# Attention and two feed-forward networks: the rational function of network 2 moved into PSUM banks, one of its products to GpSimd

## The chip, the core and the metric

One core of a Trainium2 chip runs the whole program in one launch. The metric is the device time of one execution in microseconds. TensorE (PE) multiplies matrices into PSUM, which has eight banks of 128 x 512 fp32; VectorE (DVE) and ScalarE (ACT) work elementwise on PSUM and SBUF; GpSimd (POOL) works elementwise on SBUF; SyncE (SP) issues all the transfers, one queue in program order.

## The reference, cut to what matters

```python
def reference(q, k, v, moe_*, moe2_*):
    x = attention(q, k, v)              # chunks of 64, 8 x 8 heads x 576 rows -> 4608 x 512
    h = x @ w_in;  g = relu(h) ** 2     # network 1: 512 -> 2048
    x = g @ w_out                       #            2048 -> 512
    h = x @ w_in2                       # network 2: 512 -> 2048
    P = a[0] + a[1]*h + a[2]*h**2 + a[3]*h**3
    Q = 1.0 + abs(b[0])*abs(h) + abs(b[1])*h**2
    g = P / (Q + 1e-6)
    return (g @ w_out2)                 #            2048 -> 512, 4608 x 512 out
```

## The kernel before

The 4608 rows are nine blocks of 512. Each fp32 operand is held as a high part and a low part, and each product of two of them is three matmuls of 128 x 512 (`mm3`: low by high, high by low, high by high). A "tile" is one 128 x 512 piece of h, `(b, f)` for block b and feature slice f of 16, so a network has 144 tiles; a "second product" is the 12 matmuls that take one finished tile g through `w_out` into the four `acc` banks. Network 1 runs its first product tile by tile (12 matmuls in `mm_h`), and the second product two tiles later (`mm_out1`). Network 1's last 16 second products (`BACK = 16`) are put off: their activations are kept in SBUF (`keep`, 20 slots in the space of weights that are no longer needed), the last 14 first products run back to back, and the 16 are done inside network 2.

Network 2 takes eight of the nine blocks in four pairs. For a pair `m` and a pair of feature slices `u` (a "unit", 32 of them) seven products of sums replace eight (`mm_p`, numbered 1 to 7, 6 matmuls each; the sums of weights lie in `w2q`, those of the inputs in `x2q`). From them come four tiles of h: 11 (products 1 and 2), 12, 22 and 21. Before, the order of TensorE in a unit is 1, 5, second product, 6, 2, second, 7, 3, second, 4, second, with no second products in unit 0; the ninth block follows in `mm_s2` (16 tiles of 12 matmuls, each with a second product), and the 20 second products that are left end the program.

The parts of a tile are put together so: products 1, 6, 7 and 4 go on one after the other in one bank (`h`, two buffers), 5 and 3 in `e`, 2 in `b`. ScalarE copies the running sums to SBUF where they branch off (`q_copy`: `s1`, `s5`, `sU`), VectorE adds them (`q_add`): 11 into its own bank `b`, 12 and 22 into SBUF (`h12`, `h22`); 21 is left in bank `h`. Then comes the rational function, eleven instructions a tile: ScalarE's square (L905), scaled abs (L909) and affine (`id`, L917); VectorE's denominator `t` (L913, both inputs in SBUF); ScalarE's ln and exp for the reciprocal (L921, L925); VectorE's `wh`, `wa` (L929, L933, which read h), `u` (L937, a Newton step on the reciprocal), `wr` (L941) and `g` (L944, which ends it into a kept slot). For the second product ScalarE makes the high part of g (`o_hi`, `gh`) and GpSimd the low part (`o_lo`, `gl`, L196).

For the next pair of blocks GpSimd forms the sums of the inputs from rows loaded back from DRAM: per `xq` (24 of them in network 2, eight per pair, in a pair's first five units) a load, four subtractions (L344), ScalarE's high part, GpSimd's low part (L196) and a store, in one buffer `xroom`.

The order of network 2 on all queues is made by a planner (`job`, `plan`): TensorE's order is given, every other engine takes of what is ready by the planner's own costs what is due first, and the result is a fixed order for each queue. In `issue` the events of one common list are written out in order of their time.

Of the kernel before, what the change touches and what calls it, by code (L numbers as in the profile page):

```python
# [19 lines left out]
NB = 512  # L20
# [8 lines left out]
COST = {"sq": 2.6, "abs": 3.0, "id": 3.4, "ln": 3.2, "exp": 3.2, "hi": 2.8, "cp": 2.8, "t": 3.7, "wh": 3.0, "wa": 3.3,  # L29
        "u": 3.0, "wr": 3.3, "g": 3.1, "add": 3.2, "lo": 5.7, "ev": 2.8}  # L30
# [52 lines left out]
def attn_moe_moe_kernel(  # L83
# [43 lines left out]
    h_p = ctx.enter_context(tc.tile_pool(name="hps", bufs=2, space=PSUM))  # L127
# [150 lines left out]
    def w2_parts(key, st, x):  # L278
# [9 lines left out]
        copy(nc.scalar, hi, x)  # L288
# [34 lines left out]
    def xq_room(i):  # L323
# [3 lines left out]
        z = (T["xroom"] if i >= 8 else T["room", i % 2])[:, 0:14 * 128].rearrange("p (x t j) -> p t x j", t=2, j=128)  # L327
# [42 lines left out]

    def mm_h(s):
# [6 lines left out]
        ps = h_p.tile([128, 512], F32, name="h", tag="h")  # L378
# [3 lines left out]
    def mm_h_half(s, i, k):  # L382
# [3 lines left out]
        if i == 0 and k == 0:  # L386
            T["h", s] = h_p.tile([128, 512], F32, name="h", tag="h")
# [29 lines left out]
    def mm_out2(s, g):  # L417
# [3 lines left out]
        for i in range(TPB):  # L421
# [4 lines left out]
            for j in PARTS:  # L426
                T["rest", j.start] = h_p.tile([128, 512], F32, name="h", tag="h")
# [144 lines left out]
    def mm_pv2(*ts):  # L572
        o = [h_p.tile([128, 512], F32, name="h", tag="h").rearrange("p (t b i) -> p t b i", t=2, i=64) for _ in range(2)]
# [79 lines left out]
    def g_tr(g, nm):  # L653
        x = T.pop((nm, "group", g))
        ps = h_p.tile([128, 2, 2, 128], F32, name="h", tag="h")
# [136 lines left out]
    def t2(nm):  # L792
        return tl("t2", [128, NB], F32, nm)
# [7 lines left out]
    free = list(range(20))  # L801

    def slot(i):
        return spare(i // 2)[:, i % 2]
# [18 lines left out]
    def x_page(i, c):  # L823
# [5 lines left out]
        return X[0][i - 7][:, 2 * c:2 * c + 2] if i < 9 else T["xmore"][c]  # L829
# [14 lines left out]
    def xs_hi(i, c):  # L844
        need("ring_x", i, 2)
# [7 lines left out]
    def bank(tag):  # L853
        return (h_p if tag == "h" else P["eb"]).tile([128, 512], F32, name="h", tag=tag)

    def mm_p(m, u, p):
        i, j = 7 * m + ORDER.index(p), 7 * (8 * m + u) + ORDER.index(p)
# [4 lines left out]
        tag, first = {1: "h", 5: "e", 2: "b"}.get(p), True  # L862
        if tag is None:
            tag, first = "e" if p == 3 else "h", False
        else:
            T[tag] = bank(tag)
        w = i_tile(j).rearrange("p (t k j) -> p t k j", t=2, k=2)
        x = [x_page(i, c) for c in range(2)]
        for c in range(2):
            mm3(T[tag], [([w[:, t, c] for t in range(2)], [x[c][:, t] for t in range(2)])], first and c == 0, c == 1, p in (6, 3, 7, 4))  # L870
# [5 lines left out]
    def mm_s2(f):  # L876
        u, i = divmod(f, 2)
        j = 7 * NF // 2 * (NBLK // 2) + 4 * u + 2 * i
        ps = bank("h")
# [565 lines left out]
```

## Time and profile before

| | us |
|---|---|
| median of 3 runs (lowest to highest) | 1722.89 (1719.42 to 1723.58) |
| the profiled execution, its own time | 1720.5 |
| its span, first to last instruction | 1718.7 |
| PE busy over the span | 1623.8 |
| DVE busy | 1282.6 |
| ACT busy | 983.9 |
| POOL busy | 558.2 |

The profiled execution's time is 1.8 us longer than its span and 2.4 us under the median of the runs. An engine's busy time counts its instructions alone, not its waits. An average over the span hides that the program has parts with different limits: attention and network 1 until 820 us, network 2 after that. A matmul that is listed with 0.39 us overlaps the next one; what counts is the distance from start to start. Some matmul records can be missing, so counts of them are lower bounds.

### The profile page before, as it was taken

The page shows a single profiled execution, that of the slowest core. Times are in us where ns is not written, and L with a number is a line of the kernel's source. Part 1 is how long each engine was busy: PE and PEld are TensorE (multiplying, and loading weights), DVE is VectorE, ACT ScalarE, POOL GpSimd, SP SyncE. Part 2 cuts the span into 40 slices and gives each one's busy share as a digit, 9 for nine tenths or more (in the row PEclk, how much of TensorE's full clock was granted, in tenths as well). Part 3 has the DMA queues.
Part 4 walks back from the last instruction along what each step waited for, and adds up shares of the span by engine and source line. Part 5 has one row for each costly group of instructions (what it writes and reads, how often), then busy time and mean ns, then how long its engine had stood idle before and what let it go on. Part 6 is the DMA issues. An engine that isn't in the chain of part 4 may idle for free.

```text
span 1718.7 us, 25720 instructions
## 1 busy us (share of the span) xinstructions
PE 1623.8 (94%) x9165; PEld 1323.7 (77%) x9165; DVE 1282.6 (75%) x1869; ACT 983.9 (57%) x1619; POOL 558.2 (32%) x463
## 2 busy tenths in 40 slices
PE   8999999999999999999988896999988999998999
PEld 7888778888878888888767675777766777777887
DVE  7886566666666666630799997999998999999970
ACT  6853343344333433334767775777767777777752
POOL 4640212212202112241345434552555333222233
PEclk9999999999999999999999999999999999999999
DMA  9755653444445354449868796888977886565644
GB/s 261 202 131 158 215 146 99 134 107 134 111 115 155 81 147 112 144 122 308 278 209 261 243 319 208 246 260 308 289 238 227 281 298 217 173 195 164 209 138 156
DMA packets 358871, 335.18 MB, mean 195 GB/s; under 512 B 195288, under 2 KB 269272, under 8 KB 357720
## 3 DMA queue, kind: packets, MB, share of 16 engines
q1 hardware_dynamic: 358744, 333.54, 63.7%
q8 instruction: 73, 1.20, 0.3%
q14 instruction: 54, 0.44, 0.1%
HBM read 251.66 MB, written 81.79 MB: 194 GB/s over the span
## 4 chain that ended last, share of the span: by engine, by line
PE 49%; DVE 34%; DMA 5%; ACT 4%; issue 3%; POOL 2%; SPq 1%; DVEq 0%; POOLq 0%; ACTq 0%
PE acc L367 8%; PE acc L368 8%; PE acc L369 8%; PE h L367 8%; PE h L369 7%; PE h L368 7%; DVE t L913 5%; DVE spare L944 5%; DVE w L941 4%; DVE w L929 4%; DVE w L933 4%; DVE t L937 4%; DVE at L641 3%; DVE h L898 2%; DMA x2q<-xroom 2%
## 5 line engine op out<-in xcount | busy, mean ns | idle before, releaser
L196 POOL TENSOR_TENSOR gl<-spare,gh 128x512 fp32r<-128x512 f32 x160 | 235.7, 1481 | 439.1 <-ACT gh L191 415.0
L367 PE MATMUL h<-x,w 128*128 128x512 f32 (+1 forms) x792 | 311.4, 393 | 22.1 <-ACT sU L191 10.5
L368 PE MATMUL h<-x,w 128*128 128x512 f32 (+1 forms) x792 | 308.6, 390 | 0.3 <-DVE x L196 0.3
L369 PE MATMUL h<-x,w 128*128 128x512 f32 (+1 forms) x792 | 308.5, 390 | 0.0
L367 PE MATMUL acc<-w,gl 128*128 128x512 f32 x575 | 226.8, 394 | 14.3 <-POOL gl L196 13.6
L367 PE MATMUL acc<-gh,w 128*128 128x512 f32 x576 | 227.8, 395 | 4.0 <-ACT ev L191 2.3
L368 PE MATMUL acc<-gl,w 128*128 128x512 f32 x576 | 225.1, 391 | 0.8 <-POOL gl L196 0.6
L368 PE MATMUL acc<-w,gh 128*128 128x512 f32 x575 | 225.7, 392 | 0.0
L369 PE MATMUL acc<-w,gh 128*128 128x512 f32 x575 | 225.5, 392 | 0.0
L369 PE MATMUL acc<-gh,w 128*128 128x512 f32 x576 | 224.7, 390 | 0.0
L478 ACT ACTIVATE r<-h 128x512 f32<-128x512 f32 x128 | 76.0, 594 | 208.3 <-PE h L369 148.1
L367 PEld LDWEIGHTS h<-x,w 128*128 128x128 f32 x792 | 149.7, 189 | 58.7 <-ACT sU L191 13.0
L193 DVE CAST gh<-r 128x512 fp32r<-128x512 f32 x120 | 56.6, 472 | 184.3 <-ACT r L479 183.8
L196 POOL TENSOR_TENSOR st<-wc,st 128x512 fp32r<-128x512 f32 x32 | 49.4, 1544 | 411.7 <-ACT st L191 330.4
L369 PEld LDWEIGHTS h<-x,w 128*128 128x128 f32 x792 | 149.7, 189 | 30.7
L368 PEld LDWEIGHTS h<-x,w 128*128 128x128 f32 x792 | 149.9, 189 | 30.4 <-DVE x L196 0.5
L913 DVE SCALAR_TENSOR_TENSOR t<-h,co,t 128x512 f32<-128x512 f32 x144 | 142.9, 992 | 19.0 <-ACT t L909 18.8
L921 ACT ACTIVATE r<-t,co 128x512 f32<-128x512 f32 x144 | 103.7, 720 | 82.3 <-DVE t L913 81.8
L944 DVE SCALAR_TENSOR_TENSOR spare<-t,w 128x512 f32<-128x512 f32 x144 | 128.7, 894 | 16.5 <-DVE w L941 1.4
L367 PEld LDWEIGHTS acc<-w,gl 128*128 128x128 f32 x575 | 109.3, 190 | 41.1 <-POOL gl L196 16.6
L941 DVE SCALAR_TENSOR_TENSOR w<-w,co,r 128x512 f32<-128x512 f32 x144 | 139.6, 969 | 0.0
L367 PE MATMUL h<-w,w 128*128 128x512 f32 x240 | 100.2, 418 | 41.0 <-DVE h L898 15.8
(141 smaller groups left out, 3166.3 us busy)
## 6 DMA issues: line engine op xcount, KB each, us to landing
w<-w2o SPq DMA_DIRECT2D x144, 512.0 KB, 4.9
w<-w2q SPq DMA_DIRECT2D x256, 256.0 KB, 3.9
x2q<-xroom SPq DMA_DIRECT2D x24, 896.0 KB, 5.2
st<-in_moe_w_in_dram SPq DMA_DIRECT2D x32, 512.0 KB, 4.9
st<-in_moe_w_out_dram SPq DMA_DIRECT2D x32, 512.0 KB, 5.5
w2q<-st SPq DMA_DIRECT2D x32, 512.0 KB, 2.9
w<-x2q SPq DMA_DIRECT2D x30, 512.0 KB, 8.8
x<-x2q SPq DMA_DIRECT2D x22, 512.0 KB, 8.9
```

The source lines that it names most:

```text
L196: eng.tensor_tensor(out=o, in0=x, in1=hi.bitcast(F32), op=ALU.subtract)
L367: nc.tensor.matmul(out=o, lhsT=al, rhs=bh, start=first and i == 0, stop=False, **kw)
L368: nc.tensor.matmul(out=o, lhsT=ah, rhs=bl, start=False, stop=False, **kw)
L369: nc.tensor.matmul(out=o, lhsT=ah, rhs=bh, start=False, stop=last and i == len(pairs) - 1, **kw)
L478: nc.scalar.activation(out=r, in_=ps, func=ACTF.Relu)
L913: eng.scalar_tensor_tensor(out=t, in0=T.pop(("h2", b, f)), scalar=co[:, 5:6], in1=t, op0=ALU.mult, op1=ALU.add)
L921: nc.scalar.activation(out=T["r", b, f], in_=T["t", b, f], func=ACTF.Ln, scale=2.0 ** -LN_SHIFT, bias=co[:, 6:7])
L929: nc.vector.tensor_tensor(out=w, in0=w, in1=T["H", b, f], op=ALU.mult)
L933: nc.vector.scalar_tensor_tensor(out=w, in0=w, scalar=co[:, 1:2], in1=T.pop(("H", b, f)), op0=ALU.add, op1=ALU.mult)
L937: nc.vector.scalar_tensor_tensor(out=u, in0=u, scalar=1.0 + 1e-6, in1=T["r", b, f], op0=ALU.add, op1=ALU.mult)
L941: nc.vector.scalar_tensor_tensor(out=w, in0=w, scalar=co[:, 0:1], in1=T.pop(("r", b, f)), op0=ALU.add, op1=ALU.mult)
L944: nc.vector.scalar_tensor_tensor(out=keep("g", BACK + b * NF + f), in0=T.pop(("t", b, f)), scalar=2.0, in1=T.pop(("w", b, f)), op0=ALU.sub ...
```

## The change

Nothing changes in attention and in network 1's arithmetic. In network 2:

- The four banks that the products use become four equal ones, and a table of roles (`role`, `NEXT`) says which bank serves as h, e, b or g in which unit. A branching sum is begun by a copy from bank to bank (`q_fork`: ScalarE copies product 1 from h into b; product 2 is then accumulated on it), and one sum is written by VectorE from bank h to bank e (`q_v`), on which product 3 is accumulated. One copy to SBUF (`s5`) is left. Tile 22 is written by VectorE into the bank with role g (`q_22`). So a unit has two ScalarE copies for three, and two VectorE adds for three.
- All four tiles of h stay in PSUM. The reciprocal is written by exp over h in its bank, `wr`, `u` and `g` read it there, and the bank is handed on only when `g` is done. In the tile with role g alone (`R_SB`) it is written to SBUF and the bank is free after `wa`.
- The denominator is |h| times (b1 |h| + b0): ScalarE does abs and an affine (`q_abs`, `q_lin`), and GpSimd the product (`q_q`), in place of ScalarE's square and abs and VectorE's `t`. VectorE has five instructions a tile for six.
- Every second high part of g is made on GpSimd and not on ScalarE (`"AG"[n % 2]`).
- 20 second products of network 1 are put off and not 16, all units have four second products, unit 0 too, and the order in a unit is 1, second, 5, 6, 2, second, 3, 7, second, 4, second. There are 23 kept slots, three buffers each of `r`, `t`, `w` in pools of their own, and two of `xroom`; the ring of x pages has 9 places for 10.
- The planner has other costs, due times for transfers that follow from TensorE's order, and a longer lead for a load of `xq` (`X_LAT`).
- In network 1, 48 copies that make high parts of network 2's weights go from ScalarE to GpSimd, and one activation in 16 tiles is written later.

```diff
-BACK = 16
-RING_O, RING_I, RING_X = 6, 12, 10
-ORDER = 1, 5, 6, 2, 7, 3, 4
+BACK = 20
+RING_O, RING_I, RING_X = 6, 12, 9
+UNIT_SEQ = "1o562o37o4o"
+ORDER = [int(x) for x in UNIT_SEQ if x != "o"]
+NEXT = {"h": "b", "e": "e", "b": "g", "g": "h"}
+R_SB = "g"
...
-    def q_copy(nm, tag):
-        T[nm] = tl("sx", [128, NB], F32, nm)
-        copy(nc.scalar, T[nm], T[tag])
-
-    def q_add(tag, nm, b, f):
-        o = T[tag] if tag == "b" else tl("sx", [128, NB], F32, {"e": "h12", "h": "h22"}[tag])
-        nc.vector.tensor_tensor(out=o, in0=T[tag], in1=T.pop(nm), op=ALU.add)
...
+    def q_fork(un, src, o):
+        T[o] = bank(role(un, o))
+        copy(nc.scalar, T[o], T[src])
+    def q_s5():
+        T["s5"] = tl("s5", [128, NB], F32, "s5")
+        copy(nc.scalar, T["s5"], T["e"])
+    def q_v():
+        nc.vector.tensor_tensor(out=T["e"], in0=T["h"], in1=T["s5"], op=ALU.add)
+    def q_22(un, b, f):
+        T["H", b, f] = bank(role(un, "g"))
+        nc.vector.tensor_tensor(out=T["H", b, f], in0=T["h"], in1=T.pop("s5"), op=ALU.add)
...
-    def q_t(b, f, eng):
         t = T["t", b, f]
-        eng.scalar_tensor_tensor(out=t, in0=T.pop(("h2", b, f)), scalar=co[:, 5:6], in1=t, op0=ALU.mult, op1=ALU.add)
...
+        nc.gpsimd.tensor_tensor(out=t, in0=t, in1=T["r", b, f], op=ALU.mult)
...
+    def q_exp(b, f, in_place=True):
+        r, h = T["r", b, f], T.pop(("H", b, f))
+        if in_place:
+            T["r", b, f] = h
+        nc.scalar.activation(out=T["r", b, f], in_=r, func=ACTF.Exp, scale=-1.0, bias=co[:, 7:8])
...
-            due = nominal[x] - 4
+            due = nominal[x] - 12
...
-            made["hi", n] = job("A", COST["hi"], src + prev + buf, due - 7, o_hi, n, nc.scalar)
+            eng = "AG"[n % 2]
...
+                made["hi", n] = job(eng, COST["hi"], src + prev + buf, due - 8, o_hi, n, engines[eng])
...
-                    q_ = [(made["xq", i - 1], D_LAT)] if i > 8 else []
+                    q_ = [(made["xq", i - 2], X_LAT)] if i > 9 else []
```

What stands on VectorE in the middle of network 2, before (`spare` is a kept slot, `r`, `t`, `w` are the function's own tiles, `h` with a number is a tile of h in SBUF, and `h` alone one in PSUM or SBUF):

```order
L913 SCALAR_TENSOR_TENSOR t<-h_12347,co,t 128x512
L929 TENSOR_TENSOR w<-w,h_12304 128x512
L933 SCALAR_TENSOR_TENSOR w<-w,co,h_12304 128x512
L913 SCALAR_TENSOR_TENSOR t<-h_12401,co,t 128x512
L937 SCALAR_TENSOR_TENSOR t<-t,r_12413 128x512
L941 SCALAR_TENSOR_TENSOR w<-w,co,r_12413 128x512
L944 SCALAR_TENSOR_TENSOR spare_8088<-t,w 128x512
```

And now, over two tiles, the second with role g:

```order
L946 TENSOR_TENSOR w<-w,h 128x512
L950 SCALAR_TENSOR_TENSOR w<-w,co,h 128x512
L963 SCALAR_TENSOR_TENSOR w<-w,co,h 128x512
L967 SCALAR_TENSOR_TENSOR h<-t,h 128x512
L970 SCALAR_TENSOR_TENSOR spare_7920<-h,w 128x512
L963 SCALAR_TENSOR_TENSOR w<-w,co,r 128x512
L967 SCALAR_TENSOR_TENSOR r<-t,r 128x512
L970 SCALAR_TENSOR_TENSOR spare_7920<-r,w 128x512
```

The row of `t` is gone, and of a tile's last three rows each has one operand in the bank `h` where it had two in SBUF; the tile with role g keeps two in SBUF.

On GpSimd in the same part before, only low parts and the work for the next pair of blocks stand in a row (`xroom`: sums L344 and low part L196):

```order
L196 TENSOR_TENSOR gl<-spare_8088,gh 128x512
L344 TENSOR_TENSOR xroom<-xroom 128x128 x4
L196 TENSOR_TENSOR gl<-spare_8192,gh 128x512
L196 TENSOR_TENSOR xroom<-xroom 128x7x128
L196 TENSOR_TENSOR gl<-spare_8269,gh 128x512
```

Now (L942 is the denominator's product, L199 the high part):

```order
L942 TENSOR_TENSOR t<-t,r 128x512
L350 TENSOR_TENSOR xroom_8056<-xroom_8056 128x128 x4
L202 TENSOR_TENSOR gl<-spare_8118,gh 128x512
L199 CAST gh<-spare_8190 128x512
L202 TENSOR_TENSOR xroom_8056<-xroom_8056 128x7x128
L942 TENSOR_TENSOR t<-t,r 128x512
```

The product of a tile stands behind the sums and the low part of the next pair's inputs, which begin with a load.

On TensorE, at the start of network 2, before: product 1 is followed by product 5 (`x_71` and `x_72` hold x pages, `w_0` a page of sums of weights):

```order
L367 MATMUL h<-x_71,w_0_76 128x512
L368 MATMUL h<-x_71,w_0_76 128x512
L369 MATMUL h<-x_71,w_0_76 128x512
L367 MATMUL h<-x_72,w_0_76 128x512
L368 MATMUL h<-x_72,w_0_76 128x512
L369 MATMUL h<-x_72,w_0_76 128x512
```

Now:

```order
L373 MATMUL h<-x_71,w_0_76 128x512
L374 MATMUL h<-x_71,w_0_76 128x512
L375 MATMUL h<-x_71,w_0_76 128x512
L373 MATMUL acc_580<-gh,w_4_8006 128x512
L374 MATMUL acc_580<-gl,w_4_8006 128x512
L375 MATMUL acc_580<-gh,w_4_8006 128x512
```

A second product of network 1 stands between them. In all, 48 matmuls fewer stand ahead of network 2's first.

## Rows read from the trace of the kernel before

**Rows 1.** Busy time by stretch: length, then engine busy (instructions), granted clock, DMA share, GB/s.

```profile
100.00:750.00 650.00, 642.43 (x4469) 528.13 (x4469) 408.18 (x748) 250.62 (x426) 127.14 (x111) 1.00 0.48 132
860.00:1400.00 540.00, 477.28 (x1994) 380.67 (x1993) 501.71 (x613) 391.95 (x634) 248.87 (x202) 0.97 0.81 260
1400.00:1600.00 200.00, 186.89 (x792) 151.86 (x793) 190.45 (x253) 153.86 (x251) 58.37 (x39) 0.97 0.61 198
1600.00:1714.00 114.00, 114.00 (x506) 94.53 (x505) 60.93 (x74) 57.25 (x92) 37.85 (x29) 1.00 0.48 159
```

**Rows 2.** Timeline of PE: start, length; network 2's first and last matmul.

```profile
817.81 0.39 PE L367 MATMUL h<-x,w 128*128 128x512 f32 x1
...
820.53 0.39 PE L367 MATMUL h<-x,w 128*128 128x512 f32 x1
...
1714.28 0.28 PE L369 MATMUL h<-w,gh 128*128 128x256 f32 x1
```

**Rows 3.** Waits of PE, 820 to 1719: us in total, times, longest.

```profile
PE h L367 <- ACT sU L191: 23.3, 13, 3.7
PE h L367 <- DVE h L898: 19.4, 12, 10.8
```

**Rows 4.** DVE's groups, 860 to 1500: count | busy us, mean ns | idle before.

```profile
L941 DVE SCALAR_TENSOR_TENSOR w<-w,co,r 128x512 f32<-128x512 f32 x107 | 100.4, 938 | 0.0
...
L898 DVE TENSOR_TENSOR h<-h,s 128x512 f32<-128x512 f32 x54 | 36.7, 686 | 1.8 <-PE h L369 1.8
```

**Rows 5.** Timeline of all engines, 1120 to 1125: DVE beside POOL.

```profile
1120.35 1.30 POOL L196 TENSOR_TENSOR gl<-spare,gh 128x512 fp32r<-128x512 f32 x1
...
1120.45 0.69 DVE L898 TENSOR_TENSOR h<-h,sU 128x512 f32<-128x512 f32 x1
...
1121.60 2.58 POOL L196 TENSOR_TENSOR xroom<-xroom 128x896 fp32r<-128x896 f32 x1
...
1122.11 2.62 DVE L941 SCALAR_TENSOR_TENSOR w<-w,co,r 128x512 f32<-128x512 f32 x1
```

**Rows 6.** Timeline of DVE, 1129 to 1132, where POOL does nothing.

```profile
1129.97 0.75 DVE L941 SCALAR_TENSOR_TENSOR w<-w,co,r 128x512 f32<-128x512 f32 x1
1130.83 0.69 DVE L944 SCALAR_TENSOR_TENSOR spare<-t,w 128x512 f32<-128x512 f32 x1
1131.43 0.68 DVE L929 TENSOR_TENSOR w<-w,h 128x512 f32<-128x512 f32 x1
```

**Rows 7.** ACT's groups, 860 to 1500.

```profile
L921 ACT ACTIVATE r<-t,co 128x512 f32<-128x512 f32 x107 | 77.1, 720 | 65.4 <-DVE t L913 65.0
...
L191 ACT ACTIVATE s<-h 128x512 f32<-128x512 f32 x52 | 30.0, 588 | 0.0
```

**Rows 8.** POOL's groups over the span.

```profile
L344 POOL TENSOR_TENSOR xroom<-xroom 128x128 f32<-128x128 f32 x96 | 63.8, 683 | 93.2 <-DMA xroom<-x2d 84.9 <-issue 6.4
L196 POOL TENSOR_TENSOR xroom<-xroom 128x896 fp32r<-128x896 f32 x24 | 58.8, 2449 | 15.9 <-ACT xroom L191 14.9 <-PE acc L369 1.1
...
L704 POOL TENSOR_TENSOR e<-e,z 128x512 f32<-128x512 f32 x2 | 2.1, 1044 | 11.1 <-DVE z L699 10.7 <-ACT x L191 0.4
L193 POOL CAST gh<-r 128x512 fp32r<-128x512 f32 x3 | 1.9, 639 | 6.6 <-ACT r L479 6.6
```

**Rows 9.** Timelines of SP, POOL and PE round the longest stall; in brackets idle before.

```profile
1052.36 8.23 SPq L821 DMA_DIRECT2D w<-w2q  x1
...
1068.33 1.81 POOL L344 TENSOR_TENSOR xroom<-xroom 128x128 f32<-128x128 f32 x4 [12.86 <-DMA xroom<-x2d]
...
1074.59 0.79 PE L367 MATMUL h<-w,w 128*128 128x512 f32 x1 [10.79 <-DVE h L898]
```

**Rows 10.** SP's timeline ahead of network 2, first and last loads of x pages.

```profile
798.74 0.95 SPq L839 DMA_DIRECT2D x<-x2q  x2
...
808.73 12.31 SPq L839 DMA_DIRECT2D w<-x2q  x8
```

**Rows 11.** Waits of POOL on the loads of xroom, 820 to 1600: us, times, longest.

```profile
POOL xroom L344 <- DMA xroom<-x2d: 84.9, 15, 12.9
```

More of the change, by code (lines that the diff above doesn't have):

```diff
@@ L572, in mm_pv2 @@
     def mm_pv2(*ts):
-        o = [h_p.tile([128, 512], F32, name="h", tag="h").rearrange("p (t b i) -> p t b i", t=2, i=64) for _ in range(2)]
+        o = [h_bank().rearrange("p (t b i) -> p t b i", t=2, i=64) for _ in range(2)]
         for i, t in enumerate(ts):
@@ L799, in part @@
         return ALL if i < 0 else PARTS[i]
-    free = list(range(20))
+    free = list(range(20 + MORE))
     def slot(i):
-        return spare(i // 2)[:, i % 2]
+        return spare(i // 2)[:, i % 2] if i < 20 else T["more"][:, i - 20]
     def keep(what, n):
@@ L861, in mm_p @@
         need("ring_x", i, 2)
[L862 to L866, printed above, removed]
+        tag = {2: "b", 5: "e", 3: "e"}.get(p, "h")
+        if p in (1, 5):
+            T[tag] = bank(role(un, tag))
         w = i_tile(j).rearrange("p (t k j) -> p t k j", t=2, k=2)
@@ L869, in mm_p @@
         for c in range(2):
-            mm3(T[tag], [([w[:, t, c] for t in range(2)], [x[c][:, t] for t in range(2)])], first and c == 0, c == 1, p in (6, 3, 7, 4))
+            mm3(T[tag], [([w[:, t, c] for t in range(2)], [x[c][:, t] for t in range(2)])], p in (1, 5) and c == 0, c == 1, p not in (1, 5))
+        if p == 2:
+            T["H", 2 * m + 1, 2 * u] = T.pop("b")
+        if p == 3:
+            T["H", 2 * m, 2 * u] = T.pop("e")
         if p == 4:
@@ L878, in mm_s2 @@
         j = 7 * NF // 2 * (NBLK // 2) + 4 * u + 2 * i
-        ps = bank("h")
+        ps = bank(role(NF // 2 * (NBLK // 2) - 1, "begh"[f % 4]))
         pairs = []
@@ L923, in q_exp @@
-    def q_exp(b, f):
-        r = T["r", b, f]
-        nc.scalar.activation(out=r, in_=r, func=ACTF.Exp, scale=-1.0, bias=co[:, 7:8])
+    def q_fork(un, src, o):
[9 more added lines that the diff above has]
+        nc.vector.tensor_tensor(out=T["H", b, f], in0=T["h"], in1=T.pop("s5"), op=ALU.add)
@@ new lines, in q_abs, with q_lin, q_id, q_q @@
+    def q_abs(b, f):
+        T["r", b, f] = tb("r")
+        nc.scalar.activation(out=T["r", b, f], in_=T["H", b, f], func=ACTF.Abs)
+    def q_lin(b, f):
+        T["t", b, f] = tb("t")
+        nc.scalar.activation(out=T["t", b, f], in_=T["r", b, f], func=ACTF.Identity, scale=co[:, 5:6], bias=co[:, 4:5])
+    def q_id(b, f):
+        T["w", b, f] = tb("w")
+        nc.scalar.activation(out=T["w", b, f], in_=T["H", b, f], func=ACTF.Identity, scale=co[:, 3:4], bias=co[:, 2:3])
+    def q_q(b, f):
+        t = T["t", b, f]
+        nc.gpsimd.tensor_tensor(out=t, in0=t, in1=T["r", b, f], op=ALU.mult)
@@ L1411, in attn_moe_moe_kernel @@
         pool(ctx, "eb", 1, space=PSUM)
-        T["xroom"] = tl("sx", [128, 14 * 128], F32R, "xroom")
-        T["xmore"] = [tl("sx", [128, 2, NB], F32R, f"xmore{i}") for i in range(2)]
+        for i in range(2):
+            T["xroom", i] = tl("sx", [128, 14 * 128], F32R, f"xroom{i}")
+        T["more"] = tl("sx", [128, MORE, NB], F32, "more")
         issue(3 * NS)
```

235 lines of the change are left out of this document (121 added, 114 removed), and 4 rows, old and new, of the table ON.

## The prediction

> **What bounds the kernel now.** I read first how busy the engines are by stretch [rows 1], then where network 2 begins and ends on TensorE [rows 2], what TensorE waits for there [rows 3], and last the single groups of each engine. The reader is to see that the program has two halves. In network 1 TensorE works 642 of 650 us at a granted clock of 1.00, with VectorE at 63%. From 860 to 1400 us TensorE works 477 of 540 us and VectorE 502 (93%), ScalarE 392 (73%), GpSimd 249 (46%) [rows 1]. From 1400 to 1600, where the next pair's inputs need no more sums, GpSimd falls to 29% and VectorE is still at 95%; from 1600 on, second products alone, TensorE loses nothing. So in network 2 VectorE is full and TensorE waits for what it and ScalarE, which follows it, deliver: 23.3 us for a copy of a running sum and 19.4 us for an add are its largest waits [rows 3].
>
> What is lost there. Twelve matmuls take 820.53 - 817.81 = 2.72 us when nothing waits, 0.2267 each [rows 2]. Network 2 holds 32 units x 42 matmuls + 16 x 12 + 160 second products x 12 = 3456, which is 783.4 us. It takes 1714.28 - 820.53 = 893.8 us. The difference, **110.4 us**, is idle time and the matmuls at a lower granted clock (0.97 in both VectorE-bound stretches, 1.00 before and after [rows 1]). A program whose TensorE never waited in network 2 would have a span of 1718.7 - 110.4 = 1608.3 us, and with the 1.8 us outside the span a time of **1610**. All that follows is added to that, against the profiled 1720.5, which stands 2.4 us under the median of the runs.
>
> **VectorE.** A unit is four tiles and 7 x 6 + 4 x 12 = 90 matmuls, 20.4 us of TensorE. From 860 to 1400 there are 1994 matmuls, 22.2 units, so a unit takes 24.4 us (a little less if records are missing) and VectorE works 22.6 of them. Why so long shows in the stretch at 1120: a VectorE instruction with both inputs in SBUF that meets GpSimd's 2.58 us low part takes 2.62 us, while an add with one input in PSUM takes 0.69 under a GpSimd instruction [rows 5]. Where GpSimd is idle the same kinds take 0.68 to 0.75 [rows 6]. Over the stretch the SBUF kind has a mean of 938 ns and the PSUM kind 686 [rows 4]. The change takes one of six instructions a tile away and one of three adds a unit, and gives all that are left one input in PSUM, save three in the tile with role g. A tile's five at 0.68 + 0.75 + 0.75 + 0.69 + 0.69 = 3.56 us, four tiles 14.2, two adds 1.4, evacuation copies 0.3, and for the three SBUF instructions of the g tile 3 x (0.938 - 0.75) = 0.6: **16.5 us a unit, 81% of TensorE's 20.4**. No row has an instruction that writes its result over its own input's bank; the nearest is the add at 0.69, and I take it.
>
> **ScalarE.** Five instructions a tile stay five. Abs from PSUM is like the square it replaces; the affine and exp I put at 0.72, the ln row. Exp into PSUM has no row; between 0.59 (copy out of PSUM) and 0.72 [rows 7] I take the upper. A unit loses one copy (0.59) and two high parts, which are copies too and put at the same [rows 7]: 1.8 us less, from 392 / 22.2 = 17.7 to **15.9 us, 78%**.
>
> **GpSimd** gets the product. The nearest row is a two-input fp32 multiply into fp32, 1.04 us, and a high part is like its cast, 0.64 [rows 8]. Per unit 4 x 1.30 low parts [rows 5] + 4 x 1.04 + 2 x 0.64 = **10.7 us**. The 24 sets of input sums, 4 x 0.68 + 2.45 = 5.2 us each [rows 8], fall into 15 units: 1.6 x 5.2 = 8.3 more there, **19.0 of 20.4**. This is the fullest an engine becomes, and only there.
>
> The Trainium skill (GPSIMD Engine Reference, Engine selection) speaks against this move: it sends elementwise multiplies to VectorE and calls GpSimd about twice as slow with two inputs. This trace has 1.04 against 0.69, so 1.5 times. By the page the product would be some 1.4 us (an estimate), and GpSimd would stand at 20.4 us in those 15 units, with nothing left; the sum stays, but the rival of GpSimd's queue below gains.
>
> **What remains of TensorE's waits.** All three engines now fit under 20.4 us, so TensorE sets the pace, and what is left are single waits. I bound them by how much TensorE loses beside a VectorE of a known load. At 63% (network 1) it loses 7.6 of 650 us, 1.2%; at 95% (1400 to 1600) it does 792 x 0.2267 = 179.5 us of work in 200, a loss of 10% [rows 1]. At 81%, a straight line gives 6.3%, and the lower row 1.2%. Over the 32 units, 653 us, that is 8 to 44 us. I take **28**, about the middle: the loads are nearer to 95%, but a queue's delay grows fastest just below full. The lower clock follows the waits and is contained in these shares.
>
> **The start of network 2.** Four second products of network 1 (48 matmuls, 10.9 us) move behind its start; TensorE's work in all is the same. But x pages are loaded from 798.74 on, and the last of the 14 are issued by 821 [rows 10], 1.6 us apiece; no wait for them followed. Network 2 would now begin at 809.7. In SP's order the first page's second half is the sixth load, some 808.3 when issued; the fourteenth, at 821, is wanted 16.3 us after the start, at 826, because second products now stand between. A landing takes some us more, so 0 to 8 us; I take **3**. In network 1 the 48 copies that go to GpSimd cost 48 x 0.64 = 31 us of an engine that works 127 of 650 [rows 1]; covered, nothing. If a low part in front of a second product came late by it, network 1's 7.6 us of loss bounds the scale; the later activation could as well give 2 back.
>
> Sum: 1610 + 28 + 3 = **1641**.
>
> **Rivals.** (a) *The banks are held too long.* Before, a bank went free after `wa` or an add; now after `g`. A tile's chain, abs to `g`, is 0.60 + 0.72 + 1.04 + 0.72 + 0.72 + 0.75 + 0.69 + 0.69 = 5.9 us with nothing in front. Product 5 needs the bank of the tile finished by product 3 of the unit before; between lie product 7, 4, three second products and a product 1, 12.2 us. So 6.3 us are there for queues. One other tile on ScalarE (3.5 us) and one set of input sums on GpSimd (5.2) make 8.7: 2.4 us late. Once in each of the 15 units: 36 us, **1677**. For it: in-order queues, with a tile's `ln` behind a product that stands behind those sums. Against: the other 17 units have no such sums, and there the 6.3 us suffice.
>
> (b) *GpSimd's queue becomes the chain*, which is the slower side. Before, the input sums waited for their loads 84.9 us in 15 waits [rows 11], at the worst 12.86 us behind a transfer that held SP's queue for 8.23; TensorE then stood for 10.79 [rows 9], because ScalarE's high part of those inputs stood in front. Now the product `t` stands behind those sums too. If each of the 24 sets waits the 5.7 us that 15 of them waited on average, the chain gets 5.7 + 5.2 = 10.9 us longer against 6.3 of slack: 4.6 x 24 = 110 us, **1751**. It decides from about 3.3 us a set, which is a mean wait of 4.4. Against: a second `xroom` buffer and a longer planned lead.
>
> (c) *PSUM operands don't free VectorE*, so the change doesn't do what it says: each instruction is stretched by GpSimd as L941 is. Its excess of 0.19 at GpSimd's 46% would be 0.33 at 80%: 20 x (0.71 + 0.33) + 1.7 = 22.5 us a unit, the 22.6 of now, and the time stays: **1720**. Rows 4 and 5 speak against it.
>
> (d) *Nearly all waits go*: the low end, 8 us and no loss at the start, **1618**.
>
> **How the numbers follow.** Forecast 1641, chance 0.58; (a) 0.22; (d) 0.09; (b) 0.07; (c) 0.04. The range must reach (a) with the straight-line share and the full cost at the start left open, and (d): **1616 to 1695**, which leaves out (b) and (c) and a little of (a). About 0.3% is what a measurement can tell from no change here, 5 us. Faster 0.89, same 0.04, slower 0.07.
>
> **What would show it.** Right: between 860 and 1400 (some 30 us earlier at the end) TensorE busy at 95% or more and a granted clock near 1.00; VectorE near 80%; means of `wh`, `wa` of 0.68 to 0.75 whatever GpSimd does; a GpSimd product of about 1.04. For (a): TensorE's waits before products 1 and 5 put down to VectorE's `g` row. For (b): waits for ScalarE's `ln` on GpSimd's product, in the units with input sums, and GpSimd idle on xroom's loads. For (c): means near 0.94 in instructions that read h. It would be wrong altogether if an engine's order in network 2 kept a wait for a transfer in front of the product that the planner did not foresee.

## The result, and the profile after

The changed kernel takes **1624.24 us** (median of 4 runs, 1623.48 to 1624.65) against 1722.15 of the kernel before beside it: ratio 0.9433, 95% interval 0.9416 to 0.9449, so 98 us or 5.7% less. The forecast was 1641, 17 us too long; the time lies inside the range and nearer to rival (d), 1618, than to the sum.

The busy row and the chain of waits of the changed kernel's page. Before, 49% of the chain lay on PE and 34% on DVE.

```profile
PE 1593.5 (98%) x9165; PEld 1317.5 (81%) x9165; DVE 1076.8 (66%) x1688; ACT 920.5 (57%) x1462; POOL 770.1 (47%) x737
...
PE 91%; DVE 4%; DMA 2%; ACT 1%; issue 1%; POOL 0%; SPq 0%; DVEq 0%; ACTq 0%; POOLq 0%
```

The same stretches after, with the columns of [rows 1]:

```profile
100.00:750.00 650.00, 649.50 (x4570) 537.41 (x4571) 422.33 (x762) 227.56 (x381) 151.66 (x158) 1.00 0.49 133
860.00:1400.00 540.00, 529.81 (x2325) 437.37 (x2324) 419.04 (x582) 428.03 (x661) 396.52 (x374) 0.99 0.89 293
860.00:1320.00 460.00, 449.81 (x1972) 371.10 (x1971) 357.91 (x494) 363.63 (x560) 346.55 (x331) 0.99 0.92 304
```

From 860 to 1400 TensorE issues 2325 matmuls where it issued 1994 and stands for 10.2 us of 540. VectorE went from 93% busy to 78%, with more units done in the same time; GpSimd from 46% to 73%. The DMA engines are busy for 92% of 860 to 1320: after TensorE itself they stand nearest to full there.

All of TensorE's waits from 800 to the end, which answer to [rows 3]:

```profile
PE h L373 <- DVE spare L970: 9.8, 1, 9.8
PE h L373 <- DVE h L922: 0.2, 1, 0.2
```

The list of many small waits is gone; one stall is left. Network 2's first matmul starts 0.7 us later than worked out and its last ends at 1617.85. Between them lie 3504 matmuls (the 48 that the change moved in are among them), 794.4 us at 0.2267 each, in 807.5 us: 13.1 are lost, 10.0 in those two waits and the rest where the matmuls are further apart, most of it behind the stall.

VectorE's groups from 860 to 1500, which answer to [rows 4]:

```profile
L950 DVE SCALAR_TENSOR_TENSOR w<-w,co,h 128x512 f32<-128x512 f32 x124 | 92.8, 748 | 4.4
L946 DVE TENSOR_TENSOR w<-w,h 128x512 f32<-128x512 f32 x124 | 84.6, 682 | 52.0 <-ACT w L938 52.0
L963 DVE SCALAR_TENSOR_TENSOR w<-w,co,h 128x512 f32<-128x512 f32 x93 | 69.2, 745 | 53.3 <-ACT h L959 53.3
L967 DVE SCALAR_TENSOR_TENSOR h<-t,h 128x512 f32<-128x512 f32 x94 | 64.7, 688 | 0.0
L967 DVE SCALAR_TENSOR_TENSOR r<-t,r 128x512 f32<-128x512 f32 x30 | 31.6, 1055 | 3.2
...
L970 DVE SCALAR_TENSOR_TENSOR spare<-r,w 128x512 f32<-128x512 f32 x28 | 29.8, 1065 | 1.0
L963 DVE SCALAR_TENSOR_TENSOR w<-w,co,r 128x512 f32<-128x512 f32 x30 | 27.7, 923 | 3.3 <-ACT r L959 2.9
```

The same operation at the same line has 688 ns with one operand in PSUM (`h`) and 1055 with both in SBUF (`r`, the tile with role g). ScalarE and GpSimd from 860 to 1400, against [rows 7, 8]:

```profile
L934 ACT ACTIVATE t<-r,co 128x512 f32<-128x512 f32 x104 | 84.4, 812 | 2.3
L959 ACT ACTIVATE h<-r,co 128x512 f32<-128x512 f32 x78 | 53.7, 688 | 29.8 <-DVE w L950 28.7
L959 ACT ACTIVATE r<-r,co 128x512 f32<-128x512 f32 x26 | 18.7, 720 | 0.5
...
L942 POOL TENSOR_TENSOR t<-t,r 128x512 f32<-128x512 f32 x104 | 135.4, 1303 | 67.7 <-ACT t L934 62.6 <-DVE h L926 4.2
L202 POOL TENSOR_TENSOR xroom<-xroom 128x896 fp32r<-128x896 f32 x22 | 48.5, 2205 | 1.0 <-ACT xroom L197 1.0
```

The input sums don't lie evenly: they come in bursts of eight sets, one in some 12.5 us, with none between. One burst by itself:

```profile
1170.00:1265.00 95.00, 94.93 (x419) 78.32 (x418) 78.44 (x105) 78.10 (x121) 84.46 (x85) 1.00 0.94 296
```

GpSimd is 89% busy there; between two bursts, from 1105 to 1170, it is 60% busy.

The stall that is left is of the kind of [rows 9]. Timelines after, from 1000 to 1025, of SP, POOL, ACT, DVE and PE in turn (start, length, in brackets the idle time before):

```profile
1003.19 4.96 SPq L342 DMA_DIRECT2D xroom<-x2d  x1
...
1018.20 1.81 POOL L350 TENSOR_TENSOR xroom<-xroom 128x128 f32<-128x128 f32 x4 [13.33 <-DMA w<-w2q]
1019.97 2.49 POOL L942 TENSOR_TENSOR t<-t,r 128x512 f32<-128x512 f32 x2
...
1020.04 0.95 ACT L197 ACTIVATE xroom<-xroom 128x896 fp32r<-128x896 f32 x1 [11.68 <-POOL xroom L350]
1021.27 0.72 ACT L953 ACTIVATE r<-t,co 128x512 f32<-128x512 f32 x1 [0.28 <-POOL t L942]
...
1022.75 0.75 DVE L963 SCALAR_TENSOR_TENSOR w<-w,co,h 128x512 f32<-128x512 f32 x1 [13.77 <-ACT h L959]
...
1014.65 0.39 PE L375 MATMUL acc<-w,gh 128*128 128x512 f32 x1
1024.88 0.80 PE L373 MATMUL h<-x,w 128*128 128x512 f32 x1 [9.84 <-DVE spare L970]
1025.47 0.63 PE L374 MATMUL h<-x,w 128*128 128x512 f32 x1
```

The chain of waits has that load by itself (start, length):

```profile
1003.19 14.88 DMA xroom<-x2d
```

One load of `xroom` held SP's queue for 4.96 us, and its data was there 14.9 us after the issue began, at 1018.1. GpSimd stood 13.33 us for it, with two products L942 queued behind the sums (its row names another transfer, `w<-w2q`; the chain names this one, and 1003.19 + 14.88 is 1018.07, where the row starts). ScalarE stood for GpSimd, first with the high part of those inputs and then with the `ln` (L953) of a tile; VectorE stood for ScalarE, and TensorE's product 1 stood 9.84 us for VectorE's `g`, which frees the bank. The matmuls behind it show 0.80 and 0.63 us instead of 0.39: the granted clock is 0.50 from 1024.9 to 1028.9, its lower level of 1.2 GHz, and 1.00 again from 1032 on.

The slow issue is not one into full DMA engines. The stretch of that issue alone:

```profile
1003.19:1008.15 4.96, 4.96 (x24) 4.10 (x23) 4.01 (x6) 4.42 (x7) 1.60 (x2) 1.00 0.13 51
```

The engines are 13% busy in it. It stands right behind the four stores of the first finished block of the output (`out_dram`), which held SP for 9.88 us. The kernel before has that too: 10.54 us for those four stores, 3.37 for the issue behind them. What makes these issues slow stays open.

### The profile page after: what moved, and what is told of

Read it like the earlier page. It is cut to its first block, busy times and chain, and to the rows that moved or that the text cites. A ratio compares the mean times of both kernels' runs of the same rounds, so it can differ in the third digit from the quotient of the medians.

```text
span 1622.9 us, 25746 instructions
## 1 busy us (share of the span) xinstructions
PE 1593.5 (98%) x9165; PEld 1317.5 (81%) x9165; DVE 1076.8 (66%) x1688; ACT 920.5 (57%) x1462; POOL 770.1 (47%) x737
## 4 chain that ended last, share of the span: by engine, by line
PE 91%; DVE 4%; DMA 2%; ACT 1%; issue 1%; POOL 0%; SPq 0%; DVEq 0%; ACTq 0%; POOLq 0%
PE acc L373 15%; PE acc L375 15%; PE acc L374 15%; PE h L373 15%; PE h L375 14%; PE h L374 14%; PE h L589 1%; DMA xroom<-x2d 1%; PE a L568 1%; DMA st<-in_moe_w_in_dram 1%; DVE wc L244 1%; DVE w L963 1%; DVE spare L970 0%; DMA v<-in_v_dram 0%; DVE h L967 0%
## 5 line engine op out<-in xcount | busy, mean ns | idle before, releaser
L373 PE MATMUL h<-x,w 128*128 128x512 f32 (+1 forms) x824 | 322.7, 392 | 17.9 <-DVE spare L970 9.8
L374 PE MATMUL h<-x,w 128*128 128x512 f32 (+1 forms) x824 | 321.1, 390 | 0.3 <-DVE x L202 0.3
L375 PE MATMUL h<-x,w 128*128 128x512 f32 (+1 forms) x824 | 320.9, 389 | 0.0
L942 POOL TENSOR_TENSOR t<-t,r 128x512 f32<-128x512 f32 x144 | 187.3, 1301 | 129.1 <-ACT t L934 122.3
L202 POOL TENSOR_TENSOR gl<-spare,gh 128x512 fp32r<-128x512 f32 x146 | 192.3, 1322 | 50.7 <-ACT gh L197 45.6
L199 POOL CAST st<-wc 128x512 fp32r<-128x512 f32 x32 | 21.2, 663 | 375.7 <-DVE wc L244 337.0
L373 PEld LDWEIGHTS h<-x,w 128*128 128x128 f32 x824 | 155.8, 189 | 51.9 <-DVE spare L970 10.3
L374 PEld LDWEIGHTS h<-x,w 128*128 128x128 f32 x824 | 156.0, 189 | 32.2 <-DVE x L202 0.5
L375 PEld LDWEIGHTS h<-x,w 128*128 128x128 f32 x824 | 156.0, 189 | 32.1
L199 DVE CAST gh<-r 128x512 fp32r<-128x512 f32 x117 | 58.0, 496 | 149.0 <-ACT r L489 148.3
L946 DVE TENSOR_TENSOR w<-w,h 128x512 f32<-128x512 f32 x144 | 98.3, 683 | 66.8 <-ACT w L938 66.8
L963 DVE SCALAR_TENSOR_TENSOR w<-w,co,h 128x512 f32<-128x512 f32 x112 | 83.4, 745 | 67.0 <-ACT h L959 67.0
L373 PEld LDWEIGHTS acc<-gh,w 128*128 128x128 f32 x576 | 108.2, 188 | 23.1
L375 PEld LDWEIGHTS acc<-gh,w 128*128 128x128 f32 x576 | 108.1, 188 | 22.6
```

The lines of the kernel that those rows point to most:

```text
L199: eng.tensor_copy(out=o, in_=x)
L202: eng.tensor_tensor(out=o, in0=x, in1=hi.bitcast(F32), op=ALU.subtract)
L373: nc.tensor.matmul(out=o, lhsT=al, rhs=bh, start=first and i == 0, stop=False, **kw)
L374: nc.tensor.matmul(out=o, lhsT=ah, rhs=bl, start=False, stop=False, **kw)
L375: nc.tensor.matmul(out=o, lhsT=ah, rhs=bh, start=False, stop=last and i == len(pairs) - 1, **kw)
L942: nc.gpsimd.tensor_tensor(out=t, in0=t, in1=T["r", b, f], op=ALU.mult)
```

## Experiments

Theory at their start: VectorE was the full engine, and the gain is what was taken from it, more by PSUM operands than by the product's move. Rivals: the new treatment of transfers (due times, lead, rings), or the high parts' place, brings it; the held banks cost something.

**One, before without GpSimd's reads.** GpSimd's low parts and input sums of network 2 become writes of zeros; VectorE keeps its six instructions a tile.

```diff
-        split_lo(eng, T["g", "out", n][1], slot(i), T["g", "out", n][0])
+        eng.memset(T["g", "out", n][1].bitcast(F32), 0.0)
```

> The kernel before, with one thing out: in network 2 GpSimd's low parts (of g and of the next pair's inputs) and its sums of inputs are replaced by writes of zeros of the same size, so GpSimd reads nothing there (the second product's low part and the sums are left out of the result). All orders stay. Theory A (VectorE is full because GpSimd stretches its instructions that take both inputs from SBUF): VectorE's means of L937, L941, L944 fall to 0.69 to 0.75 us, its need per unit to 4 x 4.29 + 2.05 + 0.34 = 19.6 us, under TensorE's 20.4, and the time to 1660 to 1690. Rival B (the order of the queues and the transfers made the waits): the means fall too, but TensorE waits as before, 1710 to 1722.

1635.44, ratio 0.9497 (0.9453 to 0.954): 88 us less than before without a VectorE instruction removed, more than expected. Two of VectorE's groups there, with two SBUF inputs:

```profile
L944 DVE SCALAR_TENSOR_TENSOR w<-w,co,r 128x512 f32<-128x512 f32 x102 | 76.0, 745 | 0.0
L947 DVE SCALAR_TENSOR_TENSOR spare<-t,w 128x512 f32<-128x512 f32 x102 | 71.5, 701 | 3.4
```

And its stretch in the middle of network 2, with the columns of [rows 1]:

```profile
860.00:1400.00 540.00, 524.22 (x2282) 431.37 (x2281) 467.18 (x702) 447.29 (x728) 91.00 (x217) 0.98 0.88 289
```

The instruction that took 938 ns [rows 4] takes 745. The experiment also shortens GpSimd's own work (91 us of 540 against 249), so it bounds the contention's price from above. What it gains is idle time of TensorE, 15.8 us of this stretch against 62.7; the granted clock is 0.98 against 0.97.

**Two, a control for it.** GpSimd still reads two tensors but the same one twice, so its results are zeros too.

```diff
-        split_lo(eng, T["g", "out", n][1], slot(i), T["g", "out", n][0])
+        gh = T["g", "out", n][0]
+        split_lo(eng, T["g", "out", n][1], gh.bitcast(F32), gh)
```

> The control to e1: the kernel before with the same zeros in the low parts and sums (high part minus itself, a value minus itself), but made by GpSimd's usual two-input instructions, so that GpSimd reads SBUF as before (the second product's low part and the sums of inputs are left out of the result). If the missing reads made e1 fast, this one is like before, 1712 to 1724, with VectorE's means near 0.94. If the zeros did it (through TensorE's clock), 1630 to 1660.

1677.8, ratio 0.9736 (0.9716 to 0.9755): missed. The control isn't clean: with one tensor read twice the low part takes GpSimd 1224 ns instead of 1532, and VectorE's groups become shorter with it (L941 has 911 ns where the kernel before has 972 in the same stretch). VectorE's stretch is 496.87 us for 2119 matmuls; that places it in the table below among the others. Both runs have the zeros, and the granted clock of the stretch is 0.98 in both, yet they lie 42 us apart: the zeros don't make that part. Whether they matter in the rest is not separated.

**Three, the new transfers alone on the kernel before**: two `xroom`, the ring of 9, due times, lead and planner costs.

```diff
-RING_O, RING_I, RING_X = 6, 12, 10
+RING_O, RING_I, RING_X = 6, 12, 9
...
-                    q_ = [(made["xq", i - 1], D_LAT)] if i > 8 else []
+                    q_ = [(made["xq", i - 2], X_LAT)] if i > 9 else []
```

> The kernel before with the change's treatment of transfers alone: two buffers for the next pair's inputs, nine places in the ring of x pages, due times of all loads and stores by TensorE's order, the longer lead and the new costs for the sums of inputs. No arithmetic moves. Theory A: VectorE stays at 22.6 us a unit, the single stall of 10.8 us may go, 1705 to 1722. Rival B: most of the gain is here, 1640 to 1680.

1721.72, ratio 0.9988 (0.9974 to 1.0001): nothing. VectorE is as full as before:

```profile
860.00:1400.00 540.00, 482.90 (x2022) 385.76 (x2021) 508.48 (x614) 393.36 (x637) 249.23 (x200) 0.96 0.80 264
```

So the transfers alone are not the gain. What the changed kernel would lose with the old transfers was not run. **Four, the high parts** back on ScalarE alone (`eng = "A"` for `"AG"[n % 2]`):

> The changed kernel with all high parts of g on ScalarE again, planned there. ScalarE gets 2 x 0.63 = 1.3 us more a unit (about 17.8 of TensorE's 20.4), GpSimd 1.3 less. Theory A (only VectorE was full): the time stays, 1618 to 1630. Rival D (ScalarE's load matters as much): 1640 or more.

1625.32, ratio 0.9431 (0.9412 to 0.945), the changed kernel's own time; their place doesn't matter.

**Five, the product back on VectorE.**

```diff
-        nc.gpsimd.tensor_tensor(out=t, in0=t, in1=T["r", b, f], op=ALU.mult)
+        nc.vector.tensor_tensor(out=t, in0=t, in1=T["r", b, f], op=ALU.mult)
```

> The changed kernel with the denominator's product back on VectorE (both inputs in SBUF), planned there. Theory A: VectorE needs 16.5 + 4 x 0.75 to 0.95 = 19.5 to 20.3 us a unit of TensorE's 20.4, and the loss comes back in part, 1645 to 1690. Rival B: the order and the transfers are the changed kernel's, so 1620 to 1630.

1655.69, ratio 0.9614 (0.9586 to 0.9642): the product's move is worth 31 us. Its group on VectorE, from 860 to 1400:

```profile
L942 DVE TENSOR_TENSOR t<-t,r 128x512 f32<-128x512 f32 x99 | 97.3, 982 | 9.8 <-ACT t L934 9.8
```

Its stretch:

```profile
860.00:1400.00 540.00, 515.06 (x2203) 415.93 (x2203) 489.20 (x651) 403.42 (x627) 282.51 (x261) 0.98 0.87 283
```

**Six, the reciprocal in SBUF for all roles** (`R_SB = "begh"`): the product stays on GpSimd, but three VectorE instructions of every tile have two SBUF inputs again.

> The changed kernel with exp's result of all four tiles in SBUF and not over h in its bank, so that wr, u and g read both inputs from SBUF; the banks are free after wa in all tiles. Order of GpSimd and SP unchanged. Theory A: wr, u and g go to means of 0.92 to 1.07 us, VectorE to 16.5 + 9 x 0.3 = 19.2 us a unit, and the time to 1635 to 1665. Rival C (banks held to the end of the chain cost more than the PSUM operands bring): banks come free earlier and the time stays or falls, 1612 to 1626.

1682.42 (two runs, 1676.71 and 1688.14), ratio 0.9769 (0.9688 to 0.9851): some 58 us lost, more than expected; beside a GpSimd at 79% they are longer than the 1.07 us at most that was put in. Two of their groups:

```profile
L967 DVE SCALAR_TENSOR_TENSOR r<-t,r 128x512 f32<-128x512 f32 x94 | 111.6, 1188 | 8.8 <-DVE w L963 0.5
L970 DVE SCALAR_TENSOR_TENSOR spare<-r,w 128x512 f32<-128x512 f32 x85 | 96.6, 1136 | 2.9
```

Its stretch:

```profile
860.00:1400.00 540.00, 499.04 (x2110) 403.16 (x2109) 480.75 (x530) 389.14 (x601) 427.75 (x350) 0.97 0.84 275
```

So rival (c) falls: these are the instructions that the PSUM operand keeps at 0.69.

**Seven, the bank in place for role g as well** (`R_SB = ""`), which takes the last two-input SBUF instructions away but holds role g's bank to the end.

> The changed kernel with exp over h in its bank in the fourth tile too (role g), so that no VectorE instruction of the function reads two operands from SBUF, but this bank also is held to the end of the chain. Theory A: VectorE loses another 0.6 us a unit that it did not need, no gain, 1620 to 1628. Rival C (a held bank makes TensorE wait): the copy that begins the next unit's sum waits for g, 1630 to 1680.

1634.32, ratio 0.9475 (0.9445 to 0.9505): 10 us slower though VectorE has less to do. TensorE's waits:

```profile
PE h L373 <- DVE spare L970: 10.3, 1, 10.3
PE h L373 <- ACT h L197: 6.9, 5, 1.7
```

The first row is the stall of the changed kernel. The second is new: the copy that begins a running sum waits for the held bank (ScalarE's copies stand 6.1 us for `g`, in 17 waits; in the changed kernel none does). For role g's bank rival (a) is real, at 7 to 10 us, and `R_SB = "g"` avoids it.

**Eight and nine, more VectorE work**: the last instruction of a tile twice, then three times (`for _ in range(2)`, `range(3)`).

> The changed kernel with the last VectorE instruction of each tile's function done twice (same operands, same place, the same result): 0.69 us more of VectorE a tile, 2.8 a unit, all orders unchanged. It measures the step 'what remains of TensorE's waits' by itself. VectorE's need goes from about 16.5 to 19.3 us a unit, 94% of TensorE's 20.4. By the prediction's straight line between the rows of before the loss at 94% would be some 10%, 1675 to 1695. Theory A with a sharp edge (nothing is lost until an engine's need passes TensorE's): 1624 to 1640.

1664.77, ratio 0.9651 (0.9622 to 0.968), between the two expectations.

> The same with the last instruction three times: VectorE needs 16.5 + 5.5 = 22.0 us a unit, over TensorE's 20.4. Straight line: 1690 to 1720. Sharp edge: VectorE sets the pace, 32 x (22.0 - 20.4) = 51 us over the changed kernel's 1624, 1670 to 1685.

1795.24, ratio 1.0408 (1.0376 to 1.044), far over both, and slower than before at nearly the same VectorE work a unit (22.8 us against 22.6). TensorE's largest waits:

```profile
PE h L373 <- DVE h L922: 87.9, 29, 5.9
PE h L373 <- DVE spare L972: 21.0, 15, 8.5
```

Its stretch:

```profile
860.00:1400.00 540.00, 462.29 (x1872) 364.49 (x1871) 475.01 (x634) 342.10 (x530) 349.92 (x320) 0.94 0.75 242
```

VectorE is 88% busy and TensorE waits for it. Two readings: the longer chain holds banks back, or this order doesn't let VectorE be fuller than that.

**Ten is to tell them apart**: the added work stands behind the chain, where no bank and no result waits for it.

```diff
+        for _ in range(3):
+            nc.vector.tensor_copy(out=w.bitcast(F32R), in_=w)
```

> Behind the last instruction of each tile's chain, VectorE copies that tile's numerator, which nobody reads any more, three times onto itself (one SBUF input, like the cast of 496 ns). The bank and the result are free before these copies, so the chain is no longer; only VectorE's queue is fuller: about 16.2 + 4 x 3 x 0.5 = 22.2 us a unit against TensorE's 20.4, a little under the 22.8 of the run with the last instruction three times. Theory (VectorE's load alone sets the time, and the run with the last instruction three times was slow because its load was high): VectorE busy 95% or more of 860 to 1400 and a time near the kernel before, 1700 to 1740. Rival (that run was slow because its longer chain held the banks and the results back): here 1680 to 1725 with VectorE nearly full and no large waits for the running sum's add, so about 70 to 110 us faster than that run. Second rival (any added instruction in VectorE's order delays every chain, whether the chain contains it or not): 1770 to 1800, VectorE under 90% busy, and TensorE's waits put down to the add of L922 as there.

1933.5, ratio 1.1218 (1.1194 to 1.1243), outside all three times, because the copies took 862 ns and not some 500. The marks are those of the second rival: VectorE under 90% busy, and TensorE's largest wait is for the add of L922:

```profile
PE h L373 <- DVE h L922: 154.8, 31, 9.1
```

Three of VectorE's groups from 860 to 1400:

```profile
L974 DVE CAST w<-w 128x512 fp32r<-128x512 f32 x217 | 187.1, 862 | 7.4
L963 DVE SCALAR_TENSOR_TENSOR w<-w,co,h 128x512 f32<-128x512 f32 x55 | 41.0, 745 | 23.4 <-ACT h L959 23.4
L926 DVE TENSOR_TENSOR h<-h,s 128x512 f32<-128x512 f32 x18 | 12.5, 696 | 20.3 <-PE h L375 20.3
```

Its stretch:

```profile
860.00:1400.00 540.00, 420.98 (x1632) 331.07 (x1630) 481.78 (x628) 299.53 (x466) 312.98 (x284) 0.90 0.67 213
```

VectorE's work is 26.6 us a unit here, and it is 89% busy, as in run nine (88%). The time grows from run nine by 138 us for 3.8 us more work in each of 32 units, 122 us; over 0.885 that is 137. So, as far as runs of such different load can be compared, work off the chain costs what work on it costs, and held banks are not needed to explain run nine. Of VectorE's 58 us of idle time here 44 go to two rows: it stands in its fixed order for ScalarE's exp (23.4) and for TensorE (20.3).

All runs, by VectorE's work per 90 matmuls in 860 to 1400 (its busy time over count / 90; TensorE's own is 20.4 us):

| kernel | VectorE us a unit | VectorE busy | TensorE busy | time us |
|---|---|---|---|---|
| bank in place for g | 15.1 | 71% | 97% | 1634 |
| changed kernel | 16.2 | 78% | 98% | 1624 |
| one load earlier (run twelve) | 16.2 | 78% | 99% | 1620 |
| high parts on ScalarE | 16.5 | 79% | 98% | 1625 |
| longer lead (run eleven) | 16.6 | 75% | 95% | 1650 |
| before, no GpSimd reads | 18.4 | 87% | 97% | 1635 |
| last instruction twice | 19.7 | 88% | 94% | 1665 |
| product on VectorE | 20.0 | 91% | 95% | 1656 |
| reciprocal in SBUF | 20.5 | 89% | 92% | 1682 |
| before, same tensor twice | 21.1 | 92% | 92% | 1678 |
| before | 22.6 | 93% | 88% | 1723 |
| before, new transfers | 22.6 | 94% | 89% | 1722 |
| last instruction three times | 22.8 | 88% | 86% | 1795 |
| copies behind the chain | 26.6 | 89% | 78% | 1933 |

It is a knee, not a line. In the changed order VectorE gets no fuller than 88 to 91%, in the order of before 92 to 94% (the last in run three). Up to some 0.89 x 20.4 = 18.2 us of work a unit TensorE sets the pace and loses single waits only (26 us of them in run eleven); above it the unit lasts VectorE's work divided by that share. Where the knee lies in the changed order is worked out from the share: no run of it has a load between 16.6 and 19.7 us.

**Eleven, a longer lead** for the input sums against the stall that is left (`X_LAT` 60 for 30).

> The changed kernel with the planner's lead between a load of the next pair's inputs and the sums of them at 60 for 30, so that the sums stand later in GpSimd's order. The one stall left in the changed kernel's trace (10.2 us near 1015, GpSimd waiting 13.3 us for such a load with the products behind it) should go: 1611 to 1616. If the transfers are late because all 16 DMA engines are full there, a stall stays somewhere else: 1620 to 1626.

1649.83, ratio 0.9563 (0.9541 to 0.9586): 26 us worse. That stall is gone, and others came:

```profile
PE h L373 <- DMA x<-x2q: 12.5, 2, 12.0
PE h L373 <- DVE w L946: 7.1, 1, 7.1
PE h L373 <- DMA w<-x2q: 6.1, 1, 6.1
```

All sums come later by it: the last store of `x2q` for the first of these pairs is issued at 979.4 and not at 933.7, so the x pages are late at a pair's start. **Twelve, only the second load of each pair earlier**, issued behind the first, with a lead of 60 for it alone:

```diff
+                    pre = early_load.pop(i, None)
+                    e = job("D", 3, end + q_, z + 20, xq_load, i) if pre is None else pre
+                    if m and (u, p) == (0, 7):
+                        early_load[i + 1] = job("D", 3, end + [(made["xq", i - 1], X_LAT)], z + 21, xq_load, i + 1)
-                    e = job("G", 10.5, [(e, X_LAT)], z + 60, xq_sum, i)
+                    e = job("G", 10.5, [(e, X_LAT if pre is None else 60.0)], z + 60, xq_sum, i)
```

> The changed kernel with one load a pair moved: the second load of the next pair's inputs is issued right behind the first (both buffers are free then), not one second product later behind four stores of the output. Its sum has a lead of 60 in the plan. The stall of 10.2 us near 1015 should go and nothing else move: 1610 to 1615. If that load is late because the 16 DMA engines are full after the x pages, whenever it is issued, the stall stays: 1620 to 1626.

**1620.42** (1619.7 to 1622.36), ratio 0.9406 (0.9391 to 0.9422): the fastest of all, 4 us under the changed kernel, a step about as small as can be told here, and less than expected. One stall is left here too. TensorE's wait:

```profile
PE acc L373 <- POOL gl L202: 5.1, 1, 5.1
```

A piece of the chain of waits ahead of it (start, length):

```profile
1010.77 12.45 DMA x2q<-xroom
```

And the timelines of SP and POOL there:

```profile
1011.42 8.29 SPq L831 DMA_DIRECT2D w<-w2q  x1
...
1023.28 0.58 SPq L342 DMA_DIRECT2D xroom<-x2d  x1
...
1029.59 1.81 POOL L350 TENSOR_TENSOR xroom<-xroom 128x128 f32<-128x128 f32 x4 [10.51 <-DMA xroom<-x2d]
```

The moved load does what it should: its sums begin at 1002.39 without a wait. The stall is now the third load's. It needs the buffer of the first, whose store was issued at 1010.77, behind the four stores of the output (10.36 us) and an issue of 4.92, and needed 12.45 us to land; the issue behind that store held SP for 8.29. The third load went out at 1023.28, GpSimd stood 10.51 us for it, and a low part queued behind its sums kept TensorE 5.1 us. So the stall moved and became half as long. Both versions stall behind the first stores of the output. The expectations offered full DMA engines as the reason; they are 13% busy in the issue of 4.92 us too and 77% in that of 8.29, so fullness does not explain the first, and no run tried what does.

## Why the prediction was right, and where it was off

- **The bound.** Right: VectorE was full. Taking GpSimd's reads away from the kernel before gives 88 us; putting two SBUF inputs back into the changed one costs 58, putting the product back 31. The transfers and the high parts give nothing by themselves. The copy and the add that each unit saves, the new order of a unit and the four more second products that are put off were not tried alone. One row was misread, without effect on the sum: the stretch from 1600 on is not second products alone, for the ninth block's first products run to 1657.
- **VectorE's new load.** 16.5 us was forecast, 16.2 measured. The instruction that writes over its own input's bank, which had no row, takes 688 ns. The three of role g cost more than the 938 ns put in: 1055, 1065 and 923.
- **ScalarE.** 15.9 forecast, 428.03 / 25.8 = 16.6 measured: `lin` takes 812 and `id` 763 ns where 720 was put in; exp into PSUM takes 688, under the bound taken.
- **GpSimd.** Its product was taken from the nearest row, 1.04 us, and takes 1.30. The Trainium skill (GPSIMD Engine Reference, Engine selection) calls GpSimd about twice as slow with two inputs; 1.30 against VectorE's 0.69 bears that out, and the row chosen did not. It did no harm, because the other half of the term was off the other way: the input sums fall as forecast, some 1.6 sets a unit in bursts, but a set takes 4 x 0.52 + 2.2 = 4.3 us and not 5.2. In the burst from 1170 to 1265 GpSimd needs 0.89 x 20.4 = 18.1 us a unit, where 19.0 was forecast.
- **The residual waits: the term that was mis-sized.** 28 us was read off a straight line between a VectorE at 63% and one at 95%; with the start's 3 it made 31, and 13.1 + 0.7 came. The table shows a knee in the line's place: at 78% nothing is seen to be lost to VectorE's load, and what is lost is one stall and the lower clock behind it. The lower bound of 8 was the nearer one. A line's upper point that lies behind a knee says nothing about the loads ahead of it.
- **The start of network 2, and what lies ahead of it.** 3 us were put in for late x pages, and TensorE waits for none. Its first matmul stands 0.7 us later for another reason. From 100 to 750 TensorE stands 0.5 us where it stood 7.6, and from 0 to 100 it stands 13.9 where it stood 6.3, 7.4 us of it in two waits for VectorE's `ah` (L199). "Network 1: nothing" came out by luck, then: two changes of 7 us cancel, and no run took them apart.
- **Rival (a)** left its sign once: the stall of 9.84 us is a product 1 that waits for VectorE's `g`, which holds the bank. What made `g` late is the wait for a load in (b), and no other wait for a held bank stands in the list, so it costs 9.8 us and not 36. In run seven, with role g's bank held to the end as well, it costs 7 to 10 us more.
- **Rival (b)** came true once in 24 sets: a wait of 13.33 us on the load, the product behind it, 9.84 us on TensorE. Its mechanism was described rightly, its count was not. Before there were 15 such waits [rows 11], after there is one long one.
- **Rival (c)** falls by run six. **(d)** had the nearest time, 1618, and too low a chance for a load that far below full.

## What to carry to other kernels

Work out each engine's need per unit of the engine that should set the pace, and ask how full an engine with a fixed order can get: here 88 to 94%. In these runs a load below that costs single waits only, and above it every microsecond counts in each unit. Where two engines stretch each other's instructions, moving operands (here into PSUM, by writing results over a bank that is at hand) can be worth more than moving instructions. A queue's worst case ahead of a product, not its mean load, decides what is left once nothing is full.

## What the runs showed of the hardware

- One VectorE instruction with both inputs in SBUF beside a GpSimd at 70 to 80% has a mean of 0.92 to 1.2 us, and one takes 2.50 beside a low part of `xroom` that takes 2.31. With one operand in PSUM each of them in the changed kernel's network 2 takes 0.67 to 0.75. Beside GpSimd's writes of zeros, which read nothing, the SBUF kind has means of 0.69 to 0.76. The Trainium skill (SBUF — State Buffer, Who interferes with whom) calls it an exclusive lock that two SBUF inputs contend for only against a GpSimd instruction that reads SBUF; these three rows agree.
- A cast with a single SBUF input is stretched as well: run ten's copies (L974) take 0.43 us at the least, 0.57 in the median and 2.30 at the most, with a mean of 0.86 from 860 to 1400. The same section of the Trainium skill names `cast` among the instructions that can contend, under conditions on their operands that no run here varies.
- GpSimd's two-input instruction is shorter when both inputs are the same tensor: 1224 against 1532 ns for the low part from 860 to 1400, and 1033 against 1266 for the shortest of each. What meeting VectorE adds is included in the means.
- Writing exp's result to PSUM takes ScalarE 688 ns, to SBUF 720.
- The first four stores of the output took SP 9.88 us to issue in the changed kernel, 10.54 before and 10.36 in run twelve, and the issue behind them 4.96, 3.37 and 4.92, where most others of these stretches took 0.3 to 1.3. The DMA engines were 13% busy in the issues of 4.96 and 4.92. Later blocks' four stores took 2.5 to 5.1 us in the changed kernel.
